# Placing the preparation of a spectral-filter + FFN kernel by time, with a ScalarE root, a two-tile evacuation and a split last row

## The chip, the cores and the metric

One core of one Trainium2 chip. The metric is device microseconds (us) of one execution, median over the runs of a kernel. Runs of one kernel agree within 0.2 us here, most within 0.1 or little more; a difference of 0.3 us can be read. The span of a profile is some 1.8 us shorter than the timed execution.

## The reference, cut to what matters

```python
x = A_x                                                    # [1, 2048, 512], bf16
h  = x + _A_ref(_layernorm(x), A_w_r, A_w_i)               # rfft2, times w_r + 1j*w_i, irfft2
h2 = h + _B_ref(_layernorm(h), B_w1, B_b1, B_w2, B_b2)     # relu(x@w1 + b1)**2 @ w2 + b2, inner width 1792
```

The transforms are done as matrix products with sine and cosine tables. The argument concerns the last step of the inverse transform, the second layer norm and the feed-forward network (FFN).

## The kernel before

The 2048 rows are 16 groups of 128. From about 62 us on the FFN runs over five chunks of 2, 3, 4, 4, 3 groups. While TensorE works on one chunk, the next chunk is prepared between its products: `s5` (last transform step of a group, from tile T2, four products of 256 columns; ScalarE copies half of what they give to a tile `od`), `s5b` (sum and difference of the two halves, tile R), `s6` (one product of 512 columns, and hs, the new residual), `s6b` (statistics), `rstd` (the root), `norm` (u), `transp` (u transposed into UT). Every engine carries out its instructions in the order in which they are written here; a final pass pins that order.

```python
def stage4(pr, split=False):                       # evacuates T2; split for the last round
    pt = mm_tile("p4")
    ...
    if split:
        nc.scalar.copy(dst[:, 0:2], src[:, 0:2])
        nc.vector.tensor_copy(dst[:, 2:4], src[:, 2:4])
    ...
def s6(g):
    py = bank("p6", "pp", 3)
    nc.tensor.matmul(py[:], lhsT=KI[:], rhs=Rs.pop(g)[:], start=True, stop=True)
    nc.vector.scalar_tensor_tensor(hs[:, g, :], py[:], WSC, xs[:, g, :], ALU.mult, ALU.add)

def s6b(g, on_act=False):                          # a chunk's first group on ScalarE (junk), others on VectorE
    if on_act:
        for f, sc, k in ((ACT.Copy, 1.0 / D, 0), (ACT.Square, float(D) ** -0.5, 1)):
            ...
            nc.scalar.activation(junk[:], hs[:, g, :], f, scale=sc, accum_out=mv2[:, g, k:k + 1])
    else:
        nc.vector.bn_stats(...); nc.vector.bn_aggr(...)

def rstd(a, b, on_act=()):                         # (var + eps) ** -0.5 on GpSimd
    for g in on_act:
        nc.gpsimd.tensor_tensor(nm2[:, g:g + 1], mv2[:, g, 0:1], mv2[:, g, 0:1], ALU.mult)
        nc.gpsimd.tensor_tensor(mv2[:, g, 1:2], mv2[:, g, 1:2], nm2[:, g:g + 1], ALU.subtract)
    nc.gpsimd.tensor_scalar(rs2[:, a:b], mv2[:, a:b, 1], EPS, None, ALU.add)
    nc.gpsimd.tensor_tensor(rs2[:, a:b], rs2[:, a:b], mhalf[:, 0:b - a], ALU.pow)

def prep_steps(c):
    steps = [lambda: s5(a), None, lambda: s5b(a)]
    for g in range(a, b):
        if g + 1 < b: steps.append(lambda g=g: s5(g + 1))
        steps.append(lambda g=g: s6(g))
        if g + 1 < b: steps.append(lambda g=g: s5b(g + 1))
        steps.append(lambda g=g: s6b(g, g == a))
    steps += [rstd, None, norm, None, None, transp 0, transp 1]        # shortened here

def up(f):                                         # one of 14 per chunk
    ph = bank("ph", "ph", 3)                       # three banks
    ...four products into ph...
    nc.scalar.activation(rl[:, 0:n], ph[:, 0:n], ACT.Relu, bias=b1f[:, f:f + 1], scale=1.0)
    sq = nc.vector.tensor_tensor(act[:, f, 0:n], rl[:, 0:n], rl[:, 0:n], ALU.mult)
    if f % 3 == 1 and f // 3 < b - a:              # hb = hs + b2 of group g, not before this square
        add = nc.gpsimd.tensor_tensor(hb[:, g, :], hs[:, g, :], b2b[:], ALU.add)

def down(i, f0, f1):                               # 14 products a group; at the end
    nc.vector.tensor_tensor(ot[:], po[:], hb[:, g, :], ALU.add)
    nc.sync.dma_start(ov[:, g, :], ot[:])
```

`run` deals the steps evenly over the chunk's products: after product slot k, as many steps are written as the share of time used up.

Of the kernel before, what the change touches and what calls it, by code (L numbers as in the profile page):

```python
# [34 lines left out]
def kernel(  # L35
# [37 lines left out]
    b2b = persist.tile([P, D], BF16, name="b2b")  # L73
    ident = persist.tile([P, P], BF16, name="ident")
    mhalf = persist.tile([P, 4], FP32, name="mhalf")
    ones = persist.tile([P, 512], BF16, name="ones")
    KI = persist.tile([P, P], BF16, name="KI")
    GI = persist.tile([P, 4, 256], BF16, name="GI")
# [29 lines left out]
    def mm_tile(name, dt=FP32):  # L108
        return ps.tile([P, 4096 // mybir.dt.size(dt)], dt, tag="mm", name=name)
# [34 lines left out]
    def w_reversed(i):  # L144
# [5 lines left out]
    nc.gpsimd.iota(idxL[:].rearrange("p (r e j) -> p r e j", r=2, e=2), pattern=[[0, 2], [1, 2], [2, 128]], base=1,  # L150
                   channel_multiplier=0)
    nc.gpsimd.memset(mhalf[:], -0.5)

    nc.vector.tensor_single_scalar(pI[:, 1:2], pI[:, 0:1], 3, ALU.arith_shift_right)
    nc.vector.tensor_single_scalar(pI[:, 2:3], pI[:, 0:1], 7, ALU.bitwise_and)
# [239 lines left out]

    def stage4(pr, split=False):
        Z, M = Zs.pop(pr), Ms.pop(pr)
        pt = mm_tile("p4")
        for lt in (1, 0, 3, 2):
            r, e = lt // 2, lt % 2  # L400
            if pr == 0:
                for u, k1 in ((0, 0), (1, 8)):
                    o = pt[:, 256 * lt + P * u:256 * lt + P * u + P]
                    nc.tensor.matmul(o, lhsT=Z[:, u, r, e::2], rhs=EI[:, k1, 1, :], start=True, stop=False)
                    nc.tensor.matmul(o, lhsT=M[:, u, r, e::2], rhs=EI[:, k1, 0, :], start=False, stop=True)
            else:
                o = pt[:, 256 * lt:256 * lt + 256]
                ei = EI[:, pr].rearrange("p k b -> p (k b)")
                nc.tensor.matmul(o, lhsT=M[:, 0, r, e::2], rhs=ei[:, P:3 * P], start=True, stop=False)
                nc.tensor.matmul(o, lhsT=M[:, 1, r, e::2], rhs=ei[:, 0:2 * P], start=False, stop=True)  # L410
        dst = T2[:, :, :, 2 * pr:2 * pr + 2, :]
        src = pt[:].rearrange("p (l q g s) -> p l g q s", l=4, q=2, g=G)
        if split:
            nc.scalar.copy(dst[:, 0:2], src[:, 0:2])  # L414
            nc.vector.tensor_copy(dst[:, 2:4], src[:, 2:4])  # L415
        else:
            nc.scalar.copy(dst, src)  # L417

    stage2(0, split=True)
    stage2(1)  # L420
# [7 lines left out]
    for pr in range(9):  # L428
        if 0 < pr and pr + 2 < 8:
            stage3(pr + 2)  # L430
        if pr + 3 < 8:
            stage2(pr + 3)
        if pr > 0:
            stage4(pr - 1, split=(pr == 8))
        if pr >= 5:
            warm(mm_tile("idle")[:, 0:512], 5)
        if pr < 8:
            spectral(pr)
        if pr == 0:
            table_neg((1, 3))  # L440
            tr = mm_tile("ptr", BF16)
            transposed(tr, (4, 5, 6, 7))
            table_i(tr, (4, 5, 6, 7))
        if pr == 1:
            table_neg((4, 7))
        if pr == 4:
            sin_of(GI[:].rearrange("p t c -> p (t c)"), fiI[:])
            nc.gpsimd.tensor_copy(b1f[:], b1b[:])

    ps.release()  # L450
    tab.release()
# [6 lines left out]
    hb = ffn.tile([P, G, D], FP32, name="hb")  # L458
    mv2 = ffn.tile([P, G, 2], FP32, name="mv2")
    rs2 = ffn.tile([P, G], FP32, name="rs2")  # L460
    nm2 = ffn.tile([P, G], FP32, name="nm2")

    def bank(name, tag, bufs, dt=FP32):
        return ps.tile([P, 2048 // mybir.dt.size(dt)], dt, tag=tag, name=name, bufs=bufs)
# [14 lines left out]
    def s5b(g):  # L479
        pe, od = Rs[g]  # L480
        Rs[g] = R = ffn.tile([P, 512], BF16, tag="R", bufs=3, name="R")
        nc.vector.tensor_tensor(R[:, 0:256], pe[:, 0:256], od[:], ALU.add)
        nc.vector.tensor_tensor(R[:, 256:512], pe[:, 0:256], od[:], ALU.subtract)  # L483
# [5 lines left out]

    def s6b(g, on_act=False):  # L490
        if on_act:
            for f, sc, k in ((ACT.Copy, 1.0 / D, 0), (ACT.Square, float(D) ** -0.5, 1)):
                junk = ffn.tile([P, D], BF16, tag="junk", bufs=2, name="junk")
                nc.scalar.activation(junk[:], hs[:, g, :], f, scale=sc, accum_out=mv2[:, g, k:k + 1])  # L494
        else:
            st = ffn.tile([P, 6], FP32, tag="st", bufs=4, name="st2")
            nc.vector.bn_stats(st[:], hs[:, g, :])  # L497
            nc.vector.bn_aggr(mv2[:, g, :], st[:])

    def rstd(a, b, on_act=()):  # L500
        for g in on_act:
            nc.gpsimd.tensor_tensor(nm2[:, g:g + 1], mv2[:, g, 0:1], mv2[:, g, 0:1], ALU.mult)  # L502
            nc.gpsimd.tensor_tensor(mv2[:, g, 1:2], mv2[:, g, 1:2], nm2[:, g:g + 1], ALU.subtract)
        nc.gpsimd.tensor_scalar(rs2[:, a:b], mv2[:, a:b, 1], EPS, None, ALU.add)
        nc.gpsimd.tensor_tensor(rs2[:, a:b], rs2[:, a:b], mhalf[:, 0:b - a], ALU.pow)

    CHUNKS = ((0, 2), (2, 5), (5, 9), (9, 13), (13, 16))
    us, UTs = {}, {}
# [28 lines left out]
        else:  # L537
            nc.vector.tensor_copy(dst, src)

    def prep_steps(c):  # L540

        a, b = CHUNKS[c]
        steps = [lambda: s5(a), None, lambda: s5b(a)]
        for g in range(a, b):
            if g + 1 < b:
                steps.append(lambda g=g: s5(g + 1))
            steps.append(lambda g=g: s6(g))
            if g + 1 < b:
                steps.append(lambda g=g: s5b(g + 1))
            steps.append(lambda g=g: s6b(g, g == a))  # L550
        steps.append(lambda: rstd(a, b, (a,)))
        steps.append(None)
        steps.append(lambda: norm(c, True))
        steps.append(None)
        steps.append(None)
        steps.append(lambda: transp(c, 0))
        steps.append(lambda: transp(c, 1))
        return steps

    def mlp_slots(c):  # L560
        a, b = CHUNKS[c]
        n = P * (b - a)
        UT = UTs[c]
        act = ffn.tile([P, NF, 512], BF16, tag="act", bufs=2, name="act")
        slots = []

        def up(f):
            ph = bank("ph", "ph", 3)
            for d in range(ND):
                nc.tensor.matmul(ph[:, 0:n], lhsT=W1[:, d, bass.ts(f, P)], rhs=UT[:, d, 0:n],  # L570
                                 start=(d == 0), stop=(d == ND - 1))
            rl = ffn.tile([P, 512], BF16, tag="rl", bufs=3, name="rl")
            nc.scalar.activation(rl[:, 0:n], ph[:, 0:n], ACT.Relu, bias=b1f[:, f:f + 1], scale=1.0)  # L573
            sq = nc.vector.tensor_tensor(act[:, f, 0:n], rl[:, 0:n], rl[:, 0:n], ALU.mult)  # L574
            if f % 3 == 1 and f // 3 < b - a:
                g = a + f // 3
                add = nc.gpsimd.tensor_tensor(hb[:, g, :], hs[:, g, :], b2b[:], ALU.add)  # L577
                tc.add_manual_dep(add.ins, sq.ins.name,
                                  mybir.DependencyInfo(mybir.DependencyClass.Sync, mybir.DependencyReason.DATA),
                                  reason="not before this square")  # L580

        state = {}

        def down(i, f0, f1):
            if f0 == 0:
                state[i] = bank("po", "po", 2)
            po = state[i]
            for f in range(f0, f1):
                nc.tensor.matmul(po[:], lhsT=act[:, f, bass.ts(i, P)], rhs=W2[:, f, :], start=(f == 0), stop=(f == NF - 1))  # L589
            if f1 == NF:  # L590
                g = a + i
                ot = ffn.tile([P, D], BF16, tag="ot", bufs=3, name="ot")
                nc.vector.tensor_tensor(ot[:], po[:], hb[:, g, :], ALU.add)  # L593
                nc.sync.dma_start(ov[:, g, :], ot[:])

        for f in range(NF):
            slots.append((0.22 * (b - a), lambda f=f: up(f)))
        for i in range(b - a):
            for f0, f1 in ((0, 5), (5, 10), (10, NF)):
                slots.append((0.22 * (f1 - f0), lambda i=i, f0=f0, f1=f1: down(i, f0, f1)))  # L600
        return slots

    def run(c, prep):

        slots = mlp_slots(c)
        total = sum(t for t, _ in slots)
        done, at = 0, 0.0
        for k, (t, slot) in enumerate(slots):
            slot()
            at += t  # L610
            want = len(prep) if k == len(slots) - 1 else min(len(prep), int(len(prep) * at / (total - 2.5)))
            while done < want:
                if prep[done] is not None:
                    prep[done]()
                done += 1

    s5(0)
    s5(1)
# [5 lines left out]
    s6b(0, True)  # L624
    s6(1)
    s6b(1)
    rstd(0, 2, (0,))
    norm(0, False)
    warm(idle[:], 14)
    transp(0, 0)  # L630
    transp(0, 1)
    for c in range(5):
        run(c, prep_steps(c + 1) if c + 1 < 5 else [])
    pin(tc, nc)


# [28 lines left out]
```

## Time and profile before

183.78 us (183.73 to 183.84, 4 runs). The first up product starts at 62.37 us. The prediction works out how long the products of each chunk take at pitch, which is the spacing of products in an unbroken run, and what is left as holes.

The view of waits, TensorE's alone, from 61 to 158 us of the kernel before. A line has the waiting engine, its product and line, what ended the wait, then us in total, times, longest (a wait of 0.5 us for the very first UT is left out here and below):

```profile
PE p L487 <- DVE R L483: 2.6, 4, 1.1
PE p L532 <- ACT u L517: 1.0, 3, 0.4
PE p L532 <- DVE u L520: 0.6, 2, 0.5
PE ph L570 <- ACT rl L573: 0.2, 1, 0.2
```

TensorE waits for R (s6 comes too soon after s5b) and for u (the transposes come too soon after the norm), and hardly ever for a relu (rl). That is what the change sets out to mend.

### The profile page before, as it was taken

Reading aid. Unit: us, or ns where it says so; the run is one execution under the profiler, and the core shown is the slowest. Engines: PE = TensorE matmul, PEld = TensorE weight load, DVE = VectorE, ACT = ScalarE, POOL = GpSimd, SP = SyncE. Lnnn points to the kernel's source line nnn. Section 1 sums busy time; section 2 is a strip of 40 time slices with the busy share of each in tenths; the row PEclk is TensorE's granted clock in tenths of the full one; section 3 lists DMA queues with packets and bytes.
Section 4 is the critical chain, followed back from the end, with each engine's and each line's share of the span. In section 5 each row is a group of like instructions: output and inputs, shape, how many; then the busy total and the mean of one; then the engine's idle time right before and its main releaser. Section 6 shows DMA issues by size and latency. Waiting matters only on the chain.

```text
span 181.9 us, 2667 instructions
## 1 busy us (share of the span) xinstructions
PE 160.0 (88%) x946; PEld 89.0 (49%) x946; DVE 122.2 (67%) x297; ACT 101.8 (56%) x172; POOL 46.5 (26%) x83
## 2 busy tenths in 40 slices
PE   3676896989978787999999999999999989999991
PEld 1244564666534475456643545544544434556440
DVE  7986549999957277646897248697338795359311
ACT  4976879999634278037931367922357921268200
POOL 5889910000000250204402022422022422025000
PEclk9999999999999999999999999999999999999999
DMA  5999990000000000000000000001110000110010
GB/s 159 352 425 405 378 228 23 0 0 4 2 0 0 2 4 0 2 29 29 4 0 29 29 29 4 0 0 50 36 34 0 0 0 29 58 34 0 0 58 29
DMA packets 7773, 11.19 MB, mean 62 GB/s; under 512 B 2256, under 2 KB 6224, under 8 KB 7504
## 3 DMA queue, kind: packets, MB, share of 16 engines
q1 hardware_dynamic: 7600, 10.11, 16.3%
q0 software_dynamic: 160, 0.92, 1.2%
q8 instruction: 7, 0.11, 0.3%
q14 instruction: 6, 0.05, 0.1%
HBM read 8.93 MB, written 2.10 MB: 61 GB/s over the span
## 4 chain that ended last, share of the span: by engine, by line
PE 50%; DVE 29%; ACT 9%; POOL 6%; issue 4%; DVEq 0%; POOLq 0%; ACTq 0%
PE ph L570 22%; PE po L589 20%; DVE act L574 3%; PE p L473 3%; DVE mA L379 3%; DVE mB L379 3%; DVE hs L488 2%; ACT rl L573 2%; ACT Bt L241 2%; PE p L532 2%; DVE st L497 2%; DVE st L205 2%; DVE M L392 2%; DVE Z L384 2%; ACT junk L494 1%
## 5 line engine op out<-in xcount | busy, mean ns | idle before, releaser
L570 PE MATMUL ph<-UT,W 128*128 128x384 bf16 (+2 forms) x280 | 53.2, 336 | 0.7 <-ACT UT L536 0.5
L573 ACT ACTIVATE rl<-ph,b1f 128x384 bf16<-128x384 f32 (+2 forms) x70 | 41.2, 603 | 20.9 <-PE ph L570 19.5
L589 PE MATMUL po<-W,act 128*128 128x512 bf16 x224 | 50.8, 379 | 0.0
L574 DVE TENSOR_TENSOR act<-rl 128x384 bf16<-128x384 bf16 (+2 forms) x70 | 32.5, 477 | 17.2 <-ACT rl L573 16.9
L570 PEld LDWEIGHTS <-W 128*128 128x128 bf16 x280 | 27.4, 98 | 20.8 <-issue 1.4
L589 PEld LDWEIGHTS <-act 128*128 128x128 bf16 x224 | 21.6, 98 | 27.4 <-issue 3.1
L577 POOL TENSOR_TENSOR hb<-hs,b2b 128x512 f32<-128x512 bf16 x16 | 18.4, 1153 | 57.4 <-DVE act L574 55.4
L593 DVE TENSOR_TENSOR ot<-po,hb 128x512 bf16<-128x512 f32 x16 | 11.0, 689 | 18.1 <-PE po L589 18.1
L517 ACT ACTIVATE u<-hs,nm,rs 128x512 bf16<-128x512 bf16 x6 | 4.7, 808 | 25.2 <-DVE nm L514 25.2
L231 PE MATMUL p<-KFr,xs 128*128 128x256 bf16 x28 | 8.6, 334 | 4.7 <-DVE KFr L216 4.6
L488 DVE SCALAR_TENSOR_TENSOR hs<-p,xs 128x512 bf16<-128x512 f32 x16 | 10.8, 678 | 0.1
L473 PE MATMUL p<-GI,T 128*128 128x256 bf16 x64 | 9.4, 272 | 0.4 <-DVE T L415 0.4
L502 POOL TENSOR_TENSOR nm<-mv 128x1 f32<-128x1 f32 x5 | 1.5, 291 | 30.9 <-ACT junk L494 30.9
L246 PE MATMUL idle<-ones 128*128 128x512 bf16 x37 | 9.0, 379 | 0.0
L487 PE MATMUL p<-R,KI 128*128 128x512 bf16 x16 | 6.1, 381 | 3.2 <-DVE R L483 3.2
L233 PE MATMUL p<-KFr,xs 128*128 128x256 bf16 x28 | 8.6, 335 | 0.0
L246 PEld LDWEIGHTS <-ones 128*128 128x128 bf16 x45 | 4.7, 106 | 7.8 <-POOL ones L142 2.9
L205 DVE BATCH_NORM_STATS2 st<-xs 128x6 f32<-128x512 bf16 x13 | 8.3, 673 | 0.0
L360 ACT CAST AB<-p 128x1024 bf16<-128x1024 f32 x7 | 7.1, 1014 | 1.9 <-PE p L358 1.2
L417 ACT CAST T<-p 128x1024 bf16<-128x1024 f32 x7 | 7.2, 1025 | 1.8 <-PE p L410 1.8
L330 PE MATMUL p<-GF,Bt 128*128 128x256 bf16 x64 | 8.1, 273 | 0.0
L473 PEld LDWEIGHTS <-T 128*128 128x128 bf16 x64 | 6.2, 98 | 3.5 <-ACT T L414 0.9
(135 smaller groups left out, 220.5 us busy)
## 6 DMA issues: line engine op xcount, KB each, us to landing
W<-in_B_w_dram SPq DMA_DIRECT2D x2, 1792.0 KB, 19.7
out_dram<-ot SPq DMA_DIRECT2D x16, 128.0 KB, 1.8
xs<-in_A_x_dram SPq DMA_DIRECT2D x3, 512.0 KB, 5.9
WB<-in_A_w_r_dram SPq DMA_DIRECT2D x1, 1028.0 KB, 9.6
WB<-in_A_w_i_dram SPq DMA_DIRECT2D x1, 1028.0 KB, 12.2
xs<-in_A_x_dram SPq DMA_DIRECT2D x2, 256.0 KB, 3.4
b2b<-in_B_b_dram SPq DMA_DIRECT2D x1, 128.0 KB, 8.2
b1b<-in_B_b_dram SPq DMA_DIRECT2D x1, 3.5 KB, 22.8
```

What stands on the lines that cost most here:

```text
L205: nc.vector.bn_stats(st[:], xs[:, g, :])
L231: nc.tensor.matmul(o, lhsT=xs[:, g, P * t:P * t + P], rhs=KFr[:, g, 0:P].unsqueeze(1).to_broadcast([P, 2, P]), start=True, stop=False)
L246: nc.tensor.matmul(o, lhsT=ones[:, 0:P], rhs=ones[:], start=True, stop=True)
L379: nc.vector.tensor_tensor(m[:], X[:], w[:, pr:pr + step + 1:step, 1:Df].unsqueeze(2).to_broadcast([P, 2, 2, 256]), ALU.mult)
L473: nc.tensor.matmul(pe[:, 256 - 256 * e:512 - 256 * e], lhsT=T2[:, lt, g].rearrange("p q s -> p (q s)"), rhs=GI[:, lt, :], start=(r == 0), ...
L488: nc.vector.scalar_tensor_tensor(hs[:, g, :], py[:], WSC, xs[:, g, :], ALU.mult, ALU.add)
L570: nc.tensor.matmul(ph[:, 0:n], lhsT=W1[:, d, bass.ts(f, P)], rhs=UT[:, d, 0:n], start=(d == 0), stop=(d == ND - 1))
L573: nc.scalar.activation(rl[:, 0:n], ph[:, 0:n], ACT.Relu, bias=b1f[:, f:f + 1], scale=1.0)
L574: sq = nc.vector.tensor_tensor(act[:, f, 0:n], rl[:, 0:n], rl[:, 0:n], ALU.mult)
L577: add = nc.gpsimd.tensor_tensor(hb[:, g, :], hs[:, g, :], b2b[:], ALU.add)
L589: nc.tensor.matmul(po[:], lhsT=act[:, f, bass.ts(i, P)], rhs=W2[:, f, :], start=(f == 0), stop=(f == NF - 1))
L593: nc.vector.tensor_tensor(ot[:], po[:], hb[:, g, :], ALU.add)
```

## The change

Its intent: give every step of the preparation a time, with a step of distance between producer and consumer; shorten the root; and trim the two ends of the serial path (the last evacuation of T2, the last rows). Cut to the core:

```diff
     def stage4(pr, split=False):
-        pt = mm_tile("p4")
+        pts = [mm_tile("p4a"), mm_tile("p4b")] if split else [mm_tile("p4")] * 2
...
+        if pr == 8:
+            nc.scalar.activation(junk1[:], eps[:], ACT.Sqrt, bias=eps[:])      # brings the table load here
...
-            for f, sc, k in ((ACT.Copy, 1.0 / D, 0), (ACT.Square, float(D) ** -0.5, 1)):
+            for f, sc, k in ((ACT.Copy, 1.0 / D, 0), (ACT.Square, -1.0, 1)):
+                kw = dict(bias=mv2[:, g, 0:1]) if k else {}                     # Square of (mean - x)
...
-        nc.gpsimd.... (four instructions, above)
+        nc.scalar.activation(sd2[:, a:a + 1], mv2[:, a:a + 1, 1], ACT.Sqrt, bias=eps[:], scale=1.0 / D)
+        nc.scalar.activation(sd2[:, a + 1:b], mv2[:, a + 1:b, 1], ACT.Sqrt, bias=eps[:], scale=1.0)
+        nc.vector.reciprocal(rs2[:, a:b], sd2[:, a:b])
...
-    def prep_steps(c):
+    def prep_steps(c, total):
+        gap = (total - 7.0 - t0) / (n + 1)
+        for k in range(n + 2):
+            t = t0 + k * gap
+            if k >= 2:      steps.append((t, 0.22, lambda g=a + k - 2: s6(g)))
+            if k < n:       steps.append((t, 0.44, lambda g=a + k: s5(g)))
+            if 1 <= k <= n: steps.append((t + 0.1, 0, lambda g=a + k - 1: s5b(g)))
+            if k >= 2:      steps.append((t + 0.1, 0, lambda g=a + k - 2: s6b(g, g == a)))
+        t = t0 + (n + 1) * gap
+        steps.append((t + 1.6, 0, lambda: rstd(a, b)))
+        steps.append((t + 2.2, 0, lambda: norm(c, True)))
+        steps.append((total - 2.4, 0.12 * n, lambda: transp(c, 0)))
+        steps.append((total - 1.7, 0.12 * n, lambda: transp(c, 1)))
...
+        def last(i):                                   # the last group of the last chunk
+            for h in range(2):                         # 14 products of 256 columns, then the half row goes out
```

`run` now writes a step as soon as the planned time of the products written so far has reached the step's time.

More of the change, by code (lines that the diff above doesn't have):

```diff
@@ L75 @@
     mhalf = persist.tile([P, 4], FP32, name="mhalf")
+    eps = persist.tile([P, 1], FP32, name="eps")
+    junk1 = persist.tile([P, 1], FP32, name="junk1")
     ones = persist.tile([P, 512], BF16, name="ones")
@@ L152 @@
     nc.gpsimd.memset(mhalf[:], -0.5)
+    nc.gpsimd.memset(eps[:], EPS)
     nc.vector.tensor_single_scalar(pI[:, 1:2], pI[:, 0:1], 3, ALU.arith_shift_right)
@@ L397, in stage4 @@
         Z, M = Zs.pop(pr), Ms.pop(pr)
-        pt = mm_tile("p4")
+        pts = [mm_tile("p4a"), mm_tile("p4b")] if split else [mm_tile("p4")] * 2
         for lt in (1, 0, 3, 2):
             r, e = lt // 2, lt % 2
+            pt = pts[r]
             if pr == 0:
@@ L411, in stage4 @@
         dst = T2[:, :, :, 2 * pr:2 * pr + 2, :]
-        src = pt[:].rearrange("p (l q g s) -> p l g q s", l=4, q=2, g=G)
+        src = [pt[:].rearrange("p (l q g s) -> p l g q s", l=4, q=2, g=G) for pt in pts]
         if split:
-            nc.scalar.copy(dst[:, 0:2], src[:, 0:2])
-            nc.vector.tensor_copy(dst[:, 2:4], src[:, 2:4])
+            nc.scalar.copy(dst[:, 0:2], src[0][:, 0:2])
+            nc.vector.tensor_copy(dst[:, 2:4], src[1][:, 2:4])
         else:
-            nc.scalar.copy(dst, src)
+            nc.scalar.copy(dst, src[0])
     stage2(0, split=True)
@@ L460 @@
     rs2 = ffn.tile([P, G], FP32, name="rs2")
+    sd2 = ffn.tile([P, G], FP32, name="sd2")
     nm2 = ffn.tile([P, G], FP32, name="nm2")
@@ L491, in s6b @@
         if on_act:
-            for f, sc, k in ((ACT.Copy, 1.0 / D, 0), (ACT.Square, float(D) ** -0.5, 1)):
+            for f, sc, k in ((ACT.Copy, 1.0 / D, 0), (ACT.Square, -1.0, 1)):
                 junk = ffn.tile([P, D], BF16, tag="junk", bufs=2, name="junk")
-                nc.scalar.activation(junk[:], hs[:, g, :], f, scale=sc, accum_out=mv2[:, g, k:k + 1])
+                kw = dict(bias=mv2[:, g, 0:1]) if k else {}
+                nc.scalar.activation(junk[:], hs[:, g, :], f, scale=sc, accum_out=mv2[:, g, k:k + 1], **kw)
         else:
@@ L498, in s6b, with rstd @@
             nc.vector.bn_aggr(mv2[:, g, :], st[:])
-    def rstd(a, b, on_act=()):
-        for g in on_act:
-            nc.gpsimd.tensor_tensor(nm2[:, g:g + 1], mv2[:, g, 0:1], mv2[:, g, 0:1], ALU.mult)
-            nc.gpsimd.tensor_tensor(mv2[:, g, 1:2], mv2[:, g, 1:2], nm2[:, g:g + 1], ALU.subtract)
-        nc.gpsimd.tensor_scalar(rs2[:, a:b], mv2[:, a:b, 1], EPS, None, ALU.add)
-        nc.gpsimd.tensor_tensor(rs2[:, a:b], rs2[:, a:b], mhalf[:, 0:b - a], ALU.pow)
+    def rstd(a, b):
+        nc.scalar.activation(sd2[:, a:a + 1], mv2[:, a:a + 1, 1], ACT.Sqrt, bias=eps[:], scale=1.0 / D)
+        nc.scalar.activation(sd2[:, a + 1:b], mv2[:, a + 1:b, 1], ACT.Sqrt, bias=eps[:], scale=1.0)
+        nc.vector.reciprocal(rs2[:, a:b], sd2[:, a:b])
     CHUNKS = ((0, 2), (2, 5), (5, 9), (9, 13), (13, 16))
@@ L538, in transp @@
             nc.vector.tensor_copy(dst, src)
-    def prep_steps(c):
+    def prep_steps(c, total):
         a, b = CHUNKS[c]
-        steps = [lambda: s5(a), None, lambda: s5b(a)]
-        for g in range(a, b):
-            if g + 1 < b:
-                steps.append(lambda g=g: s5(g + 1))
-            steps.append(lambda g=g: s6(g))
-            if g + 1 < b:
-                steps.append(lambda g=g: s5b(g + 1))
-            steps.append(lambda g=g: s6b(g, g == a))
-        steps.append(lambda: rstd(a, b, (a,)))
-        steps.append(None)
-        steps.append(lambda: norm(c, True))
-        steps.append(None)
-        steps.append(None)
-        steps.append(lambda: transp(c, 0))
-        steps.append(lambda: transp(c, 1))
+        n = b - a
+        t0 = 0.3
+        gap = (total - 7.0 - t0) / (n + 1)
+        steps = []
+        for k in range(n + 2):
+            t = t0 + k * gap
+            if k >= 2:
+                steps.append((t, 0.22, lambda g=a + k - 2: s6(g)))
+            if k < n:
+                steps.append((t, 0.44, lambda g=a + k: s5(g)))
+            if 1 <= k <= n:
+                steps.append((t + 0.1, 0, lambda g=a + k - 1: s5b(g)))
+            if k >= 2:
+                steps.append((t + 0.1, 0, lambda g=a + k - 2: s6b(g, g == a)))
+        t = t0 + (n + 1) * gap
[3 more added lines that the diff above has]
+        steps.append((total - 1.7, 0.12 * n, lambda: transp(c, 1)))
         return steps
@@ L582, in mlp_slots @@
         state = {}
+        def last(i):
+            g = a + i
+            ot = ffn.tile([P, D], BF16, tag="ot", bufs=3, name="ot")
+            for h in range(2):
+                po = bank("po", "po", 2)
+                sl = slice(256 * h, 256 * h + 256)
+                for f in range(NF):
+                    nc.tensor.matmul(po[:, 0:256], lhsT=act[:, f, bass.ts(i, P)], rhs=W2[:, f, sl], start=(f == 0),
+                                     stop=(f == NF - 1))
+                nc.vector.tensor_tensor(ot[:, sl], po[:, 0:256], hb[:, g, sl], ALU.add)
+                nc.sync.dma_start(ov[:, g, sl], ot[:, sl])
         def down(i, f0, f1):
+            if c == 4 and i == b - a - 1:
+                return last(i) if f0 == 0 else None
             if f0 == 0:
@@ L601, in mlp_slots, with run @@
         return slots
-    def run(c, prep):
+    def run(c):
         slots = mlp_slots(c)
-        total = sum(t for t, _ in slots)
-        done, at = 0, 0.0
+        prep, at = [], 0.0
+        if c + 1 < 5:
+            n = CHUNKS[c + 1][1] - CHUNKS[c + 1][0]
+            prep = prep_steps(c + 1, sum(t for t, _ in slots) + 0.9 * n)
         for k, (t, slot) in enumerate(slots):
@@ L610, in run @@
             at += t
-            want = len(prep) if k == len(slots) - 1 else min(len(prep), int(len(prep) * at / (total - 2.5)))
-            while done < want:
-                if prep[done] is not None:
-                    prep[done]()
-                done += 1
+            while prep and (prep[0][0] <= at or k == len(slots) - 1):
+                _, cost, piece = prep.pop(0)
+                piece()
+                at += cost
     s5(0)
@@ L626 @@
     s6b(1)
-    rstd(0, 2, (0,))
+    rstd(0, 2)
     norm(0, False)
@@ L632 @@
     for c in range(5):
-        run(c, prep_steps(c + 1) if c + 1 < 5 else [])
+        run(c)
     pin(tc, nc)
```

## The prediction

> **What bounds the kernel now.** I read the page first (shares, slices), then the busy times by stretch, the chain of work that ended last, the waits, and last the timeline around each wait.
>
> ```profile
> PE 160.0 (88%) x946; PEld 89.0 (49%) x946; DVE 122.2 (67%) x297; ACT 101.8 (56%) x172; POOL 46.5 (26%) x83
> PE   3676896989978787999999999999999989999991
> 52.00:62.40 10.40, 8.40 (x49) 4.15 (x49) 5.41 (x13) 3.25 (x8) 1.35 (x4) 1.00 0.00 1
> 62.40:78.70 16.30, 13.97 (x103) 9.38 (x103) 10.88 (x31) 9.19 (x23) 3.82 (x6) 1.00 0.01 2
> 102.70:130.40 27.70, 27.70 (x150) 13.79 (x148) 18.09 (x40) 14.12 (x25) 6.42 (x8) 1.00 0.06 19
> ```
>
> The first two lines are TensorE's share and its 40 slices; the others are a stretch, its length, and busy us of PE, weight loads, DVE, ACT, POOL. From 62.4 us on, the MLP runs over five chunks of 2, 3, 4, 4, 3 row groups; under each the next chunk is prepared (s5, s6, statistics, norm, transposes). TensorE bounds it, with holes early and none in chunk 2. Busy time flatters it, so I count products at the pitch they reach in unbroken runs of the chain: 512 wide 0.2157 us (28 in 6.04), 384 wide 0.1625 (56 in 9.10), 256 wide 0.11 (4 in 0.44), 128 wide 0.056 (8 in 0.45). Chunk 0 is then 56x0.109 + 28x0.2157 + 12x0.11 + 3x0.2157 + 12x0.056 = 14.8 us; likewise 21.7, 27.7, 26.8, 18.2. From first up product to first up product the timeline has 18.1, 24.0, 27.7, 27.6, 18.3 (62.37, 80.48, 104.49, 132.17, 159.81, 178.14). Holes: 3.3, 2.3, 0.0, 0.8, 0.1, together 6.5 us: all that better placing can win.
>
> Before the MLP there is one serial passage, where the chain holds every link:
>
> ```profile
> 53.11 0.59 ACT T L414
> 53.72 0.70 DVE T L415
> 54.56 0.61 PE p L473 x4
> 55.20 0.38 ACT od L476
> ...
> 57.72 1.34 ACT junk L494 x4
> 59.48 0.24 POOL rs L504
> 59.80 0.73 POOL rs L505
> 60.56 0.74 DVE u L520 x2
> ```
>
> VectorE evacuates its half of T2 only after ScalarE's, and the root is two GpSimd instructions between statistics and norm. Columns: start, length, what.
>
> **What the Trainium skill says.** "PSUM — Partial Sum Buffer", the section on bank collisions: two engines may not touch the same PSUM bank and quadrant at once, so accesses have to be ordered. The halves lie in different banks of one tile; that the order goes by tile is my reading. The trace agrees that two tiles are free of it: in the split of stage 1, ScalarE starts at 21.50 and VectorE at 21.64. "ScalarE: Activation LUTs", "What ACT_TABLE_LOAD costs": a load of about 1283 ns plus a drain of about 1380 ns for a switch, and under "Table sets" relu, copy and identity are in every set. The first load here is 1.28 us; what follows it waits for VectorE anyway, so the drain isn't shown. The built order has just one more load, ahead of the first Sqrt. "SBUF — State Buffer", "Who interferes with whom": a VectorE instruction with two SBUF inputs and a GpSimd instruction that reads SBUF exclude each other for the whole instruction. The trace agrees: squares (0.42 alone) that meet the hb addition end 0.29 us after it.
>
> **The change part by part.**
>
> *T2 in two tiles.* The halves run side by side: VectorE would start at 53.11, after the last product, and end 0.6 us sooner. ScalarE's half can start near 52.6, ends near 53.2; the table load of 1.28 and a tiny Sqrt (0.25) then hold it until 54.7, while od is wanted at 54.6. Gain 0.5 us; if the drain is real, it becomes a loss of about 0.8.
>
> *Root by Sqrt, first chunk.* Out: four GpSimd instructions, of which 59.06 to 60.56 lie on the path, 1.5 us. In: Square now takes the mean as bias and must wait for it (0.72 instead of 0.61 and no overlap, as the pair of the first layer norm at 7.52 shows: +0.25), two Sqrt (about 0.45) and a reciprocal (0.2). Gain 0.55.
>
> *Last rows in halves.* The last addition is 256 wide, 0.41 (the R row's shape) instead of 0.69; the products cost 28x0.11 against 14x0.2157, +0.06. The smaller write may give 0.1. Gain 0.3.
>
> *FFN preparation.* The built order gives s5, R and s6 a step each, and puts more behind the up products. It removes waits of s6 for R. But on ScalarE the two statistics passes (junk) now stand directly behind their hs addition, after square 8; before, two relus stood between:
>
> ```profile
> 111.47 0.77 DVE L574 TENSOR_TENSOR act<-rl 128x512 bf16<-128x512 bf16 x1 [0.74 <-ACT rl L573]
> 112.16 0.68 DVE L488 SCALAR_TENSOR_TENSOR hs<-p,xs 128x512 bf16<-128x512 f32 x1
> 112.69 0.69 ACT L573 ACTIVATE rl<-ph,b1f 128x512 bf16<-128x512 f32 x1 [0.18 <-PE ph L570]
> 113.28 0.62 ACT L494 ACTIVATE junk<-hs 128x512 bf16<-128x512 bf16 x1
> 114.50 0.67 ACT L573 ACTIVATE rl<-ph,b1f 128x512 bf16<-128x512 f32 x1
> ```
>
> Here hs ends at 112.84 and ScalarE reaches junk at 113.28 without idling. Walk chunk 2 of the new order by hand with these lengths, from its first up product (an up group is 0.863; an engine starts 0.27 after its producer group ends):
> up group 8 ends 8.65; relu 8 runs 8.92 to 9.61. Square 7 ends 9.20, so the hb addition holds the port from 9.28 to 10.43, and square 8 ends 10.72. hs(9) ends 11.32. ScalarE is free from 9.93 and waits 1.4 us for it. junk (1.46 a pair, as at 6.78 to 8.24) ends 12.83, relu 9 at 13.5. There are three ph banks, so up group 12 needs relu 9; it was due at 11.89: TensorE loses 1.6 us. At the end, s6(12) is followed by 19 down products (4.1 us) before the transposes: hs, statistics, Sqrt and reciprocal take 2.4, then an ot addition (0.65) that stands ahead of nm, then nm and two ScalarE norms (1.7), in all 4.8 with latencies: 0.7 lost. Chunk 2: 30.0 against 27.7, worse by 2.3.
> The same walk for the others. Chunk 1: 1.5 lost behind junk, 0.25 on R, 0.75 at the transposes: 24.2, worse by 0.2 (before, it lost 1.4 at the transposes, where the root's 1.5 us on GpSimd lay). Chunk 0: 0.5 at R, 1.7 behind R and junk, 0.3 at the transposes: 17.3, better by 0.8. Chunk 3: the last three up groups are already covered by the three banks when junk runs, after relu 10: no loss, 26.8, better by 0.8. Chunk 4: unchanged. Together +0.9 us.
>
> Sum: 183.8 - 0.5 - 0.55 - 0.3 + 0.9 = 183.3 us.
>
> **The rivals.** *The holes close.* If junk does not hold the relus, because hs comes sooner or the square does not collide with the hb addition (each collision is 0.85), chunks 0 to 2 give back up to 1.5 us each: 179 to 181 us. For it: this is what the change is meant to do, the waits of TensorE for R in the profile are real (3.2 us), and the root leaves the path to every transpose. Against: ScalarE's and VectorE's programs are in order, and hs and junk stand side by side in them. *The table switch costs its drain:* +1.3 us, 184.6. Against: nothing in the trace after the first load shows it. *Nothing moves,* as the holes only change owner: 183 to 184, close to my walk.
>
> **Range and chances.** The walk is good to some 2 us, as a shift of one square against one GpSimd addition moves a chunk by 0.8. An author who placed steps by time will have meant to close holes, so I lean 0.7 us below the sum: 182.6, range 180.2 to 184.7. Faster by over 2% means under 180.1, which needs over half of the 6.5 us besides the 1.3 at the ends: 0.16. Slower by over 2% means over 187.5: 0.04.
>
> **What would show it.** T2's two evacuations overlap, one table load near 53.2 us and od by 54.8; first up product at 61.3. In chunks 1 and 2 a wait of ScalarE's junk for hs of about 1 us and of TensorE's up product for a relu of 1.5 us; waits at the transposes of 0.7; chunk lengths 17.3, 24.2, 30.0, 26.8, 18.3. No GpSimd rs. Wrong if chunk 2 stays at 27.7, or if the first up product comes after 62.

## The result, and the profile after

182.3 us (182.25 to 182.37, 4 runs) against 183.78: ratio 0.992, 95% interval 0.9903 to 0.9937. A ratio is the mean time of one kernel's runs over that of the other's of the same rounds, so it is not quite the ratio of the medians quoted. The gain of 1.5 us is clear of the noise.

| stretch | before | predicted | after |
|---|---|---|---|
| first up product at | 62.37 | 61.3 | 61.55 |
| chunk 0 | 18.1 | 17.3 | 16.84 |
| chunk 1 | 24.0 | 24.2 | 23.95 |
| chunk 2 | 27.7 | 30.0 | 29.79 |
| chunk 3 | 27.6 | 26.8 | 26.80 |
| chunk 4 | 18.2 | 18.3 | 18.20 |

(For chunk 4 the prediction has 18.3, as it took the modelled end of the last product; the other two are taken at pitch.) Chunks 0 to 3 together took 97.44 us before and 97.38 after. So nearly the whole gain lies at the two ends: the FFN starts 0.82 us earlier, and the last row gives some 0.5 (0.52 in a4, below). What the chunks won and lost cancels.

The timeline of the serial passage after (start, length, engine, line, operation, tiles and shapes; in brackets the idle time before and what ended it), to set beside the chain shown in the prediction:

```profile
52.68 0.59 ACT L418 CAST T<-p4a 128x512 bf16<-128x512 f32 x1 [1.42 <-PE p4a L414]
52.92 1.24 PE L249 MATMUL idle<-ones 128*128 128x512 bf16 x5
53.12 0.69 DVE L419 CAST T<-p4b 128x512 bf16<-128x512 f32 x1 [1.03 <-PE p4b L414]
53.29 1.28 ACT L454 ACT_TABLE_LOAD   x1
54.22 1.03 PE L480 MATMUL p<-GI,T 128*128 128x256 bf16 x8
54.58 0.29 ACT L454 ACTIVATE junk<-eps 128x1 f32<-128x1 f32 x1
54.90 0.77 ACT L483 COPY od<-p 128x256 f32<-128x256 f32 x2
...
57.42 0.63 ACT L502 ACTIVATE junk<-hs 128x512 bf16<-128x512 bf16 x1 [1.76 <-DVE hs L495]
59.02 0.29 ACT L510 ACTIVATE sd<-mv,eps 128x1 f32<-128x1 f32 x1
59.23 0.28 ACT L511 ACTIVATE sd<-mv,eps 128x1 f32<-128x1 f32 x1
59.54 0.17 DVE L512 RECIPROCAL rs<-sd 128x2 f32<-128x2 f32 x1 [0.61 <-ACT sd L511]
59.74 0.74 DVE L527 TENSOR_SCALAR u<-hs,mv,rs 128x512 bf16<-128x512 bf16 x2
```

The evacuations now overlap and VectorE's ends at 53.81 instead of 54.41, but od starts only 0.3 us earlier than before (54.90 for 55.20). From junk to the first norm it is 2.32 us; before, from 57.72 to 60.56, it was 2.84.

TensorE's waits after, in the same view and stretch as before (its kernel's line numbers differ: L494 is s6, L539 the transposes, L581 the up products):

```profile
PE ph L581 <- ACT rl L584: 2.9, 3, 1.4
PE p L494 <- DVE R L490: 1.1, 3, 0.5
PE p L539 <- ACT u L524: 0.7, 2, 0.4
```

The waits for R fell from 2.6 to 1.1 us and those for u in the chunks from 1.2 to 0.7. (The two lines for u before add up to 1.6, but 0.47 of that is the serial passage's, at 61.03 us; its like after, 0.45 us, comes at 60.21 and so outside the window.) In their place stands a wait for a relu, 2.9 us in three pieces. The timeline of chunk 2, which had no hole before, shows how one comes about:

```profile
111.55 1.16 POOL L588 TENSOR_TENSOR hb<-hs,b2b 128x512 f32<-128x512 bf16 x1 [1.88 <-DVE act L585]
111.90 1.08 DVE L585 TENSOR_TENSOR act<-rl 128x512 bf16<-128x512 bf16 x1 [0.44 <-ACT rl L584]
112.91 0.68 DVE L495 SCALAR_TENSOR_TENSOR hs<-p,xs 128x512 bf16<-128x512 f32 x1
113.62 0.63 ACT L502 ACTIVATE junk<-hs 128x512 bf16<-128x512 bf16 x1 [1.41 <-DVE hs L495]
115.09 2.47 ACT L584 ACTIVATE rl<-ph,b1f 128x512 bf16<-128x512 f32 x4
115.81 1.02 PE L581 MATMUL ph<-UT,W 128*128 128x512 bf16 x4 [1.42 <-ACT rl L584]
```

Read it from the bottom. TensorE's up product at 115.81 idled 1.42 us for the relu that frees one of three ph banks. That relu stands behind junk in ScalarE's order. junk waited 1.41 us for hs. hs waited for a square (act) that took 1.08 us instead of 0.42, because an hb addition ran on GpSimd from 111.55 to 112.71 (b2, below, tests this). Counted at pitch, the hole before that up product is 1.59 us: the 12 products from 111.63 on would have ended at 114.22, and the 1.42 us start from a modelled end.

At the end of the same chunk the norm waits behind an ot addition that VectorE has to make first:

```profile
128.05 0.18 DVE L512 RECIPROCAL rs<-sd 128x4 f32<-128x4 f32 x1 [0.37 <-ACT sd L511]
128.16 0.69 DVE L618 TENSOR_TENSOR ot<-po,hb 128x512 bf16<-128x512 f32 x1
128.77 0.15 DVE L521 SCALAR_TENSOR_TENSOR nm<-mv,rs 128x4 f32<-128x4 f32 x1
...
130.53 0.90 PE L539 MATMUL p<-ident,u 128*128 128x128 bf16 x13 [0.25 <-ACT u L524]
```

ScalarE's two norms, 1.52 us from 128.96 on, could not begin before nm. The 16 transposes started at 129.95, and the next product followed them at 131.27: 1.32 us for 0.90 us of work, so 0.42 us lost.

The profiled execution granted TensorE a lower clock in two early slices (mean 0.981). That costs nothing: timed runs at mean clocks 0.98 and 1.0 took 182.26 and 182.37 us.

### The profile page after: what moved, and what is told of

It is laid out like the page before. It is cut to its first block, busy times and chain, and to the rows that moved or that the text cites. A ratio compares the mean times of both kernels' runs of the same rounds, so it can differ in the third digit from the quotient of the medians.

```text
span 180.5 us, 2670 instructions
## 1 busy us (share of the span) xinstructions
PE 159.4 (88%) x960; PEld 90.5 (50%) x960; DVE 126.7 (70%) x303; ACT 107.3 (59%) x184; POOL 38.6 (21%) x64
## 4 chain that ended last, share of the span: by engine, by line
PE 50%; DVE 29%; ACT 11%; POOL 4%; issue 3%; DVEq 0%; POOLq 0%; ACTq 0%
PE ph L581 22%; PE po L614 18%; ACT junk L502 3%; DVE act L585 3%; DVE hs L495 3%; DVE mA L382 3%; DVE mB L382 3%; PE p L480 3%; ACT rl L584 2%; ACT Bt L244 2%; PE p L539 2%; PE po L602 2%; ACT u L524 2%; DVE st L208 2%; DVE M L395 2%
## 5 line engine op out<-in xcount | busy, mean ns | idle before, releaser
L581 PE MATMUL ph<-UT,W 128*128 128x384 bf16 (+2 forms) x280 | 51.9, 336 | 3.4 <-ACT rl L584 2.9
L585 DVE TENSOR_TENSOR act<-rl 128x384 bf16<-128x384 bf16 (+2 forms) x70 | 34.5, 514 | 20.7 <-ACT rl L584 19.9
L614 PE MATMUL po<-W,act 128*128 128x512 bf16 x210 | 48.0, 379 | 0.0
L581 PEld LDWEIGHTS <-W 128*128 128x128 bf16 x280 | 27.4, 98 | 23.9 <-issue 4.7
L614 PEld LDWEIGHTS <-act 128*128 128x128 bf16 x210 | 20.4, 98 | 23.9 <-DVE act L585 0.4
L511 ACT ACTIVATE sd<-mv,eps 128x2 f32<-128x2 f32 (+2 forms) x5 | 1.5, 294 | 24.6 <-DVE mv L506 24.6
L618 DVE TENSOR_TENSOR ot<-po,hb 128x512 bf16<-128x512 f32 x15 | 10.3, 689 | 7.8 <-PE po L614 7.2
L244 ACT CAST Bt<-p 128x1024 bf16<-128x1024 f32 x7 | 6.8, 1009 | 1.8 <-PE p L236 1.8
L489 DVE TENSOR_TENSOR R<-p,od 128x256 bf16<-128x256 f32 x16 | 6.6, 414 | 1.6 <-ACT od L483 1.6
```

The lines of the kernel that those rows point to most:

```text
L244: nc.scalar.copy(dst, pt[:].rearrange("p (e i q s) -> p e i q s", e=4, i=2, q=16))
L581: nc.tensor.matmul(ph[:, 0:n], lhsT=W1[:, d, bass.ts(f, P)], rhs=UT[:, d, 0:n], start=(d == 0), stop=(d == ND - 1))
L614: nc.tensor.matmul(po[:], lhsT=act[:, f, bass.ts(i, P)], rhs=W2[:, f, :], start=(f == 0), stop=(f == NF - 1))
```

## The experiments

Twelve kernels, each beside runs of the kernel before on the same chip (the b runs were made on another chip than the a, c, d and e runs). All were correct. A negative difference is faster.

| run | what it is | us | against |
|---|---|---|---|
| a1_two_tiles | before + two tiles | 183.37 | before (183.72) -0.35, ratio 0.9981 |
| a2_sqrt_root | before + Sqrt root | 182.39 | before -1.33, 0.9927 |
| a3_placed_by_time | before + placement | 184.88 | before +1.16, 1.0063 |
| a4_last_halves | before + halves | 183.20 | before -0.52, 0.9971 |
| b1_junk_later | after, junk later | 180.07 | after (182.3) -2.2 |
| b2_hb_late | after, hb late | 180.40 | after -1.9 |
| b3_front | after, load early, 3 warm-ups | 181.95 | after -0.35 |
| b4_norm_at_root | after, norm at the root | 181.28 | after -1.0 |
| c1_all | after, all four repairs | 178.03 | before (183.73) -5.7, 0.9689 |
| d1_old_placement | after, old placement | 181.52 | after -0.8; before -2.2, 0.9879 |
| d2_old_mended | d1 + three repairs | 180.23 | d1 -1.3 |
| e1_chunk0_stats | c1, the junk under chunk 0 moved to VectorE | 177.38 | before (183.72) -6.3, 0.9654 |

The kernel after did not run in the later rounds; differences to it are taken by medians. The kernel before read 183.68 to 183.78, so that adds at most 0.1 us.

### One part at a time

**a1_two_tiles**

```diff
-        pt = mm_tile("p4")
+        pts = [mm_tile("p4a"), mm_tile("p4b")] if split else [mm_tile("p4")] * 2
```

> The kernel before with only the two-tile evacuation of T2. My theory: the two evacuations overlap and VectorE's ends near 53.8 instead of 54.4 us, but the five warm-up products that stand ahead of s5 on TensorE run until about 54.2, so s5 starts 0.34 us earlier and not 0.6, and nothing else waits (no table load here): 183.4 us, 0.3 to 0.4 us faster. Rival (the evacuations decide alone): 0.6 us faster, 183.2. Rival (the table load was what cost the rest in the changed kernel): od would start well before 54.86, at about 54.6.

Measured -0.35 us, as expected. This kernel has no second table load, and od still starts at 54.88, so the load did not decide it; and s5 starts 0.4 us after VectorE's evacuation has ended (53.80), so that did not either:

```profile
54.21 1.03 PE L474 MATMUL p<-GI,T 128*128 128x256 bf16 x8
54.88 0.76 ACT L477 COPY od<-p 128x256 f32<-128x256 f32 x2 [1.63 <-PE p L474]
```

What is left are the five warm-up products that stand before s5 in TensorE's order; b3 tests them.

**a2_sqrt_root**: the root and the Square with bias, and the early tiny Sqrt, in the kernel before (the diff lines of the change above).

> The kernel before with only the root by ScalarE Sqrt and reciprocal. My theory: the table load (1.28 us) follows the T2 copy on ScalarE and delays the first od by about 0.1 us; from junk to the first norm 2.3 us instead of 2.84; and at the transposes of chunks 0 and 1, where TensorE lost about 0.45 and 1.0 us behind the root on GpSimd, 0.4 and 0.7 us come back; Square with its bias costs ScalarE 0.24 us a chunk, some 0.2 us in all. 182.5 us, 1.3 us faster (0.8 to 1.7). Rival (only the first chunk's chain is on the path): 0.4 us faster, 183.4. Rival (the switch costs a drain as well): no gain or slower.

Measured -1.33 us. The first up product came at 61.89 (0.48 us sooner), chunk 0 took 17.69 (-0.4), chunk 1 23.39 (-0.6), chunk 2 27.68, chunk 3 27.87 (+0.2). So the root is worth more in the chunks (0.8 us net) than on the serial passage (0.48): TensorE's waits for u in the chunks fell from 1.2 to 0.3 us, while those for R rose from 2.6 to 3.0. In this kernel the load ran from 53.76 and od started at 55.25, 0.05 us later than before: the load was nearly hidden.

**a3_placed_by_time**: the new `prep_steps` and `run` in the kernel before.

> The kernel before with only the placement by time; the root stays on GpSimd (two or four instructions, 1.5 us between statistics and norm instead of about 0.65). My theory: in this order only 19 down products (4.1 us) lie between the last s6 and the transposes, so that the root's extra 0.85 us falls on TensorE in chunks 0, 1 and 2, and the junk pair holds the relus as in the changed kernel: slower than before by 2 us, 185.8 us (185 to 186.5). Rival (the placement by itself is what gains, as it removes waits of s6 for R): faster than before, 181.5 to 183.

Measured +1.16 us: slower, so the rival falls, but by less than I expected (184.88, just under my range). Chunks: 17.42, 24.19, 30.03, 26.96, against 16.84, 23.95, 29.79, 26.80 with the Sqrt root. The GpSimd root cost 0.58 us more only in chunk 0, and 0.24, 0.24, 0.16 in the others. My 0.85 us each was too much. The timeline of chunk 2 of this run shows one reason: the ot addition, which follows the root in the changed kernel, runs beside it here:

```profile
129.44 0.69 DVE L597 TENSOR_TENSOR ot<-po,hb 128x512 bf16<-128x512 f32 x1 [0.36 <-PE po L593]
129.56 1.04 POOL L505 TENSOR_TENSOR rs<-rs,mhalf 128x4 f32<-128x4 f32 x1
130.63 0.17 DVE L514 SCALAR_TENSOR_TENSOR nm<-mv,rs 128x4 f32<-128x4 f32 x1 [0.50 <-POOL rs L505]
```

From the end of the statistics to nm it is 1.56 us here and 1.08 in the changed kernel, 0.48 more and not 0.85. Why only 0.24 of that reaches the chunk was not traced.

**a4_last_halves**: `last(i)` in the kernel before.

> The kernel before with only the last rows in halves. My theory: last addition 0.42 instead of 0.69 us, a 64 KB write that lands 0.3 us sooner, products 0.06 us longer: 0.5 us faster, 183.3 us. Rival (the write's fixed time decides, the addition overlaps it): within 0.1 us of before.

Measured -0.52 us. The DMA lines of the page, before and after (KB each, us from issue to landing), hold the part that the prediction had too small:

```profile
out_dram<-ot SPq DMA_DIRECT2D x16, 128.0 KB, 1.8
```

```profile
out_dram<-ot SPq DMA_DIRECT2D x2, 64.0 KB, 1.5
```

**d1_old_placement**: the changed kernel with the old `prep_steps` and `run`.

> The changed kernel with the placement of the kernel before; two tiles, Sqrt root and halves stay. My theory (the placement by time loses what it gains, net 0.8 us, because junk holds the relus and ot stands ahead of nm): chunks 17.7, 23.4, 27.7, 27.8 us as in the run with Sqrt alone, 181.5 us, 0.8 us faster than the changed kernel. Rival (the placement is a gain that the single run hid, because the GpSimd root does not suit it): slower than the changed kernel.

Measured 181.52 us, as expected, 0.8 us faster than the changed kernel. Two tiles, root and halves alone add up: 0.35 + 1.33 + 0.52 = 2.2 us, and this kernel, which has just these three, is 2.21 us faster than before. Its chunks are those of a2 (17.69, 23.40, 27.68, 27.87). So the placement, the main part of the change, lost 0.8 us as it stood.

### What the placement loses, and how to get it back

**b1_junk_later**

```diff
-            steps.append((t + 0.1, 0, lambda g=a + k - 2: s6b(g, g == a)))
+            steps.append((t + 0.1 + (lag if k == 2 else 0), 0, lambda g=a + k - 2: s6b(g, g == a)))
+        steps.sort(key=lambda s: s[0])          # lag: two up groups
```

> The changed kernel, but the two statistics passes on ScalarE (junk) come two up groups later, so that relus run while hs is awaited. My theory: TensorE's 2.9 us of waits for a relu in chunks 0, 1 and 2 go, the waits for R (1.1 us) stay: 2 to 2.9 us faster than the changed kernel, 179.4 to 180.3 us; chunk 2 near 28.4 us. Rival (VectorE's backlog is the bound, so that the wait only moves to the down products or the transposes): less than 1 us faster.

Measured -2.2 us; chunk 2 took 28.46. ScalarE's timeline in chunk 2 of this run: two relus, then junk, which no longer idles.

```profile
111.87 0.69 ACT L585 ACTIVATE rl<-ph,b1f 128x512 bf16<-128x512 f32 x1 [0.49 <-PE ph L582]
112.74 0.69 ACT L585 ACTIVATE rl<-ph,b1f 128x512 bf16<-128x512 f32 x1 [0.18 <-PE ph L582]
113.32 0.62 ACT L502 ACTIVATE junk<-hs 128x512 bf16<-128x512 bf16 x1
```

TensorE's waits for a relu are down from 2.9 to 0.5 us (chunk 0 keeps one); those for R are 1.3 (1.1 in the changed kernel).

**b2_hb_late**

```diff
-            if f % 3 == 1 and f // 3 < b - a:
-                g = a + f // 3
+            for g in range(a, b) if f == NF - 1 else ():       # all behind the last square
```

> The changed kernel, but all additions hb on GpSimd wait for the chunk's last square, so they run beside the down products, where VectorE has no instruction with two inputs in SBUF. My theory (the port that GpSimd and VectorE share stretches the squares, and hs with them): no square is longer than 0.45 us in chunk 2, hs of the first row group ends 0.7 to 0.85 us sooner, the wait of TensorE for a relu falls from 1.4 to about 0.6 us in chunk 2 and vanishes in chunk 1, the waits for R vanish: 2 to 3 us faster than the changed kernel, 179.3 to 180.3 us. Rival (the stretched squares cost nothing): within 0.3 us of the changed kernel.

Measured -1.9 us, just short of my range. The 28 squares of 512 columns took 0.424 us on average instead of 0.579 (0.537 in the kernel before: there the squares were stretched too, but two relus stood between hs and junk), and hs of chunk 2's first prepared group ended 10.59 us after the chunk's start instead of 11.25. The timeline of chunk 2 in this run:

```profile
110.85 0.42 DVE L585 TENSOR_TENSOR act<-rl 128x512 bf16<-128x512 bf16 x1 [0.44 <-ACT rl L584]
...
111.91 0.63 ACT L502 ACTIVATE junk<-hs 128x512 bf16<-128x512 bf16 x1 [0.76 <-DVE hs L495]
114.11 1.02 PE L581 MATMUL ph<-UT,W 128*128 128x512 bf16 x4 [0.78 <-ACT rl L584]
```

The wait of junk and with it that of TensorE is 0.65 us shorter; the waits for R fell to 0.2 us. Waits for a relu remain in all three chunks (0.93, 0.48 and 0.78 us), 2.2 us in all, where I had counted on about 1.5: I had expected the one in chunk 1 to vanish.

**b3_front**

```diff
-        if pr == 8:
+        if pr == 6:
             nc.scalar.activation(junk1[:], eps[:], ACT.Sqrt, bias=eps[:])
-            warm(mm_tile("idle")[:, 0:512], 5)
+            warm(mm_tile("idle")[:, 0:512], 3 if pr == 8 else 5)
```

> The changed kernel, but the table load for Sqrt is made two rounds earlier, where ScalarE is idle, and three warm-up products instead of five stand ahead of s5. My theory: s5 starts when T2 is there, near 53.85, and od near 54.5 instead of 54.9: 0.35 us faster than the changed kernel, 181.95 us. Rival (s5 waits for something else): no change. Rival (a cold TensorE from fewer warm-up products): slower.

Measured -0.35 us, to 181.95. s5 now waits for VectorE's half of T2 (53.78), and od starts 0.3 us sooner:

```profile
53.93 1.03 PE L480 MATMUL p<-GI,T 128*128 128x256 bf16 x8 [0.23 <-DVE T L419]
54.61 0.77 ACT L483 COPY od<-p 128x256 f32<-128x256 f32 x2 [1.37 <-PE p L480]
```

The run changes two things at once. With the load in its old place ScalarE would be taken until 54.87 (54.58 and 0.29), so fewer warm-up products alone could not have brought od to 54.61. The load lies in a gap of ScalarE, and the next instruction follows at once:

```profile
48.72 1.28 ACT L454 ACT_TABLE_LOAD   x1
50.01 0.29 ACT L454 ACTIVATE junk<-eps 128x1 f32<-128x1 f32 x1
```

**b4_norm_at_root**: `norm` at t + 1.6, with `rstd`, instead of t + 2.2.

> The changed kernel, but nm and the norm follow the root at once on VectorE, ahead of the ot addition that stands between them in chunks 1 and 2. My theory: u is ready 0.7 us sooner there; TensorE's loss at those transposes (0.8 and 0.6 us) goes: 1.2 us faster than the changed kernel, 181.1 us (180.9 to 181.6). Rival (the ScalarE norms, 1.5 us for two, decide alone): under 0.4 us faster.

Measured -1.0 us: chunk 1 23.45 (-0.5), chunk 2 29.36 (-0.43), and TensorE has no wait for u left. In chunk 1 nm now starts 0.21 us after the reciprocal does (98.47 after 98.26), and ot comes after u, at 99.20; in chunk 2 of the changed kernel, above, it was 0.72.

### Repairs together, and the old placement with them

**c1_all**: b1 + b2 + b3 + b4.

> The changed kernel with the four repairs together: junk two up groups later, hb additions after the chunk's last square, table load early with three warm-up products, norm at once after the root. My theory: the gains of the parts (2.2, 1.9, 0.35, 1.0 us) overlap only where junk and hb shorten the same wait for a relu; nearly all of TensorE's holes close: chunks near 16.0, 22.0, 27.8, 26.8 us, in all 177 us (176.5 to 178). Rival (VectorE, which carries the most after TensorE, becomes the bound): 178.5 us or more.

Measured 178.03 us, a hair over my range: chunks 16.2, 22.35, 28.03, 26.8. The repairs sum to 5.5 us singly and give 4.3 together. Most of the difference is in chunk 2: b1, b2 and b4 took 1.33, 0.73 and 0.43 us off it singly, 2.49 in all, and together 1.76. There junk and hb shorten the same wait; that this is the reason is read from the single runs, as no run has just these two. Of what is left over the products alone, 2.4 us, chunk 0 has 1.4, with a wait of 0.5 us for a relu among it.

**d2_old_mended**: d1 with hb late, the load early and the norm at the root.

> The old placement with the other parts, and three of the four repairs (hb late, table load early, norm at once after the root; junk already has relus between it and hs there). My theory: squares are not stretched, so R comes sooner, but R still is asked for one up group or less after its evacuation, so some waits for R stay: chunks 17.2, 22.4, 27.7, 27.4 us, 179.2 us (178.5 to 180). Then the placement by time, once mended, is worth some 2 us. Rival (the placement does not matter once the squares are free): within 0.7 us of the placement by time with its repairs.

Measured 180.23 us, outside my range; I had expected 179.2. Chunks 17.47, 23.27, 27.68, 27.21. TensorE still waits 1.9 us for R in four places:

```profile
PE p L494 <- DVE R L490: 1.9, 4, 1.1
```

The old order asks for R too soon even when the squares are not stretched. So the rival falls, and the placement by time is worth 2.2 us once its faults are mended (180.23 against 178.03). It was a loss of 0.8 as it stood.

**e1_chunk0_stats**

```diff
-  s6b(g, g == a)
+  s6b(g, g == a and c != 1)                    # and one Sqrt with scale 1.0 for that chunk
```

> The repaired kernel (four repairs), but the statistics of chunk 1's first row group are taken by VectorE too, so ScalarE has no junk pair (1.46 us) under chunk 0. My theory (in chunk 0 ScalarE, with its relus of 0.42 us each beside up groups of 0.44, is what holds TensorE): the wait of 0.5 us for a relu goes, VectorE gets 0.7 us more and keeps some of it: chunk 0 near 15.9 instead of 16.2 us, 177.7 us. Rival (VectorE's row of squares, R, hs and statistics is the bound): chunk 0 as long or longer, 178.0 to 178.4.

Measured 177.38 us (5 rounds), 0.65 less than c1_all and 0.3 less than expected: chunk 0 took 15.59 us. VectorE got more work and the chunk became shorter, so in chunk 0, with its narrow products, it was ScalarE that held TensorE. In the view of TensorE's waits the wait for a relu is gone; 0.4 us for R, 0.2 for u, 0.2 for a square and the 0.5 for the very first UT are left.

This is the fastest kernel, 3.5% under before and 2.7% under after (177.38 against 182.3).

## Why the prediction was right, point by point

- **The size and its signs.** The sum said 183.3, the stated time was 182.6, measured 182.3. The sum was 1.0 us too high, because the walk by hand was too pessimistic: by 0.46, 0.25 and 0.21 us in chunks 0, 1 and 2. The start came 0.25 us later than summed and the end gained 0.2 us more, which cancel. The lean of 0.7 toward the author's intent was a guess that happened to point the right way.
- **Chunk 2 gets worse.** Predicted +2.3 us, measured +2.1. Step by step: hs of its first group was to end 11.32 us after the chunk's start and ended at 11.25; ScalarE was to wait 1.4 us for it and waited 1.41; TensorE was to lose 1.6 us and lost 1.59, counted at pitch as the prediction counts (an up product due at 11.88 started at 13.47); the transposes were to lose 0.7 and lost 0.42. b1 shows that junk's place carries the wait for the relu (with junk later, chunk 2 has none), b2 that the stretched square makes up 0.65 us of it, and b4 that the ot addition ahead of nm is what costs at the transposes (0.43 us back).
- **Chunk 1, right by luck.** It was to lose 1.5 us behind junk, 0.25 for R and 0.75 at the transposes, 2.5 in all. At pitch it lost 0.75, 0.90 (0.68 and 0.22) and 0.62, 2.27 in all. So the sign "a wait for a relu of 1.5 us" failed here (the view has 0.59), and the term for R was too small by nearly as much as that for junk was too large.
- **Chunk 0.** It was to lose 2.5 us: 0.5 for R, 1.7 behind R and junk, 0.3 at the transposes. At pitch it lost 2.06: 1.08 for the relu, 0.86 for R in two pieces, and 0.1 at the transposes.
- **T2 in two tiles.** Right that VectorE's half ends 0.6 us sooner; the gain of 0.5 us was mis-sized, it is 0.35. I held the table load to be what is left in the way. It leaves ScalarE free at 54.87, but a1, which has no such load, gains no more: the step I missed is TensorE's own order, in which the warm-up products come before s5. b3 takes both away and gains 0.35 us more. (od at 54.90 also missed the sign "by 54.8" by a little.)
- **The root.** From junk to norm 0.52 us are gained, predicted 0.55. The gain at the transposes, which I had folded into the walk, is larger (a2: 0.8 us net).
- **The drain of the table switch.** The rival with a loss of 0.8 us falls: 0.01 us after the load ends, the next instruction starts (b3, and in the changed kernel 54.57 to 54.58).
- **The halves.** Predicted 0.3, measured 0.52: the term for the smaller write was 0.1 and is 0.3 (1.8 to 1.5 us to landing).
- **The shared port.** What "SBUF — State Buffer", "Who interferes with whom" of the Trainium skill says is borne out by b2: with hb moved to where VectorE's long instructions read one tile from SBUF, the squares fall back to their own length, and 1.9 us come back.
- **Rivals.** "The holes only change owner" is nearest to what happened: the waits for R and u became 2.0 us shorter, that for a relu 2.7 longer, and the chunks as a whole kept their length (97.44 and 97.38 us).
- **Two figures that do not hold.** A collision of a square with an hb addition was put at 0.85 us; in chunk 2 it moved hs by 0.66 (11.25 against 10.59 in b2). And the chance of a gain over 2% was said to need over half of the 6.5 us besides the 1.3 at the ends; 183.8 less 180.1 is 3.7, less 1.3 is 2.4, about a third. So the bar behind the 0.16 was set too high.

What is left in e1_chunk0_stats against the products alone, counted at pitch in its trace: in chunk 0 0.8 us (0.35 for R, 0.39 for u), in chunk 1 0.7 (0.39 for R, the rest in two small pieces), in chunk 2 0.4 (a square before a down product). No run was made to close these.

## What to carry to other kernels

When work is interleaved by time, distance between producer and consumer has to be kept on every engine's queue, not only on the bound one's: a consumer placed directly behind its producer (junk behind hs) blocks everything that the same engine owes the bound engine, and the number of buffers limits how long that may last (with three ph banks, the repair by two up groups was enough in chunk 2). Before counting on a gain at the head of a chain, read what else the releasing engine has in its queue; warm-up or filler work counts. And test a many-part change part by part: here the smaller parts earned 2.2 us and the main part lost 0.8, until four small edits turned it into a gain of 2.2.

## What the Trainium skill lacked or had wrong

- "ScalarE: Activation LUTs", "What ACT_TABLE_LOAD costs": the load of about 1283 ns agrees (1.28 us in every run), the further 1380 ns of drain for a switch does not show: the next ScalarE instruction starts 0.01 us after the load (54.57 to 54.58; 50.00 to 50.01), and in the changed kernel the load starts 0.02 us after the copy before it ends (53.27 to 53.29).
- "PSUM — Partial Sum Buffer", bank collisions: the rule is by bank and quadrant. In the kernel before, two halves of one tile (128x512 f32 each) are nevertheless evacuated one after the other (53.11 and 53.72), with VectorE idle until ScalarE's copy ends; two tiles go together (52.68 and 53.12). That is on no page. a1, which changes the tiles alone, shows that the order of this program goes by tile.
- "SBUF — State Buffer", "Who interferes with whom": right, but it gives no time for this pair of instructions. Here an addition of 1.16 us on GpSimd stretched a square of 0.42 us to 1.08 (it ended 0.27 us after the addition), and the hb additions stretched the 28 wide squares from 0.424 to 0.579 us on average.
- No page has a figure for a power on GpSimd: 0.73 us for two columns, 1.04 for four, against 0.5 us for two Sqrt and 0.17 for the reciprocal that replace it.
